# First batch with keys in one run, sums in matmuls of their own, first weights by quarters, and another order

## The chip, the cores and the metric

The kernel runs on one core of a Trainium2 chip. Its time is the device time of one execution in microseconds (us); three runs before the change gave a median of 164.9 (164.26 to 165.55).

## What is computed

```python
# q, k, v: (4, 8, 768, 64); block 32, window 16, nb = 24
k_sum = k.reshape(B, H, nb, block, D).max(axis=3)
v_sum = v.reshape(B, H, nb, block, D).mean(axis=3)
scores_l = scale * (q @ k.T)               # kept where |i - j| < window
scores_s = scale * (q @ k_sum.T) + log(block)
a = softmax(concat(masked scores_l, scores_s))
x = a @ concat(v, v_sum)                   # to (3072, 512)
out = maximum(x @ w1, x @ w2) @ w_out      # w1, w2: (512, 1024)
```

The mean times 32 equals the sum, so the factor log(32) is carried by a column of 32s beside the sums of v. The maximum is computed as relu(x(w2 - w1)) + x w1, so that out = relu(x wd) w_out + x (w1 w_out).

## The kernel before

**Tiles of work.** A batch has 768 rows, taken in three groups of 256 (`grp`), and 8 heads, taken in pairs (`hp`, 0 to 3); two pairs make a half. 64 neighbouring rows see 96 keys of their own (two windows' overhang) and the 24 key sums, so one score product has 128 rows of the array: 96 keys and 32 places for sums.

**Preparing keys** (`prep`, L594). k and q of a pair are loaded (L428), cast to `kqb` with pairs of bf16 interleaved (L593 is the helper of all copies), turned on TensorE (L624), and copied by "place k" into `kx`. There each window of 64 rows has 128 columns: 64 keys, the 32 following ("tails k"), and the 24 sums ("sums k", from the maximum of L650 in `ks`). "wrap k" copies the first 32 keys behind the last ones. One product per window (`scores`, L673, matmuls at L701) then gives both kinds of score. For some pairs of the batches 2 and 3 a DMA transpose takes the place of the turn (L628).

**Preparing values** (`load_v`, `cast_v`, `spread_v`, `sums_v`). v is loaded in 64-column pieces (L470) and cast into `vx`, which has two layouts of rows: even tiles as loaded, and odd tiles shifted by 64 rows through three copies ("odd v", parts 0 to 2). The block sums come from matmuls with `amean` (L523 for the first batch, L569 later) and are copied into rows 96 to 127 of the even layout and 32 to 63 of the odd one ("all sums"). In the first batch they go by way of two `apart` tiles: the first group of rows takes them in matmuls of their own with `apart` (L762), the other groups from `vx`.

**Weighing and values.** In the first batch the mask is laid under the scores by a matmul with `hide` ("cover", L690); later batches multiply by `mask` after the exponential (L725). The exponential is on ScalarE (L715), the products with `vx` at L757, then 1/sum (L813) and its product (L816, tile `xs`). `xs` is turned into `xt` on TensorE in the first batch (L831) and by a DMA transpose (L822) later.

**Weights and output.** w1 and w2 come in four pairs of loads of 512 KB (`load_w12`, L852). Pair n holds two of the four 128-row parts of the inner dimension, and one half of the 1024 columns. Each pair gives `wd` (the difference, L856), a bf16 cast `w1b`, its turn (L869) and `w1t`. w1o = w1 w_out is made by eight products (L897). `maxout` makes for each group four hidden products (L913), relu (L922 on ScalarE, L924 on VectorE), and for each 128 rows an output product in three parts: x with w1o (L940) and two halves of g with wo (L947); then a copy and a store. Hidden product n takes quarter (2, 0, 3, 1)[n] of the columns; n = 1 and 3 need `wd[1]` and `wd[3]`, n = 0 and 2 need `wd[0]` and `wd[2]`.

**The order.** Every operation is a numbered task, in the order in which the program creates it. Three written-out lists decide the rest: CFG["order"] is the sequence in which tasks are given out (each engine and SP's DMA queue works its own through in this sequence), CFG["engines"] has a letter per task (T TensorE, D VectorE, A ScalarE, P GpSimd, S the DMA queue of SP), and CFG["slots"] the place that each new buffer takes in its ring. The ring `land`, where loads arrive, has 13 places; a load waits in SP's queue until the last user of its place is done. On TensorE the first tasks are 14 warm-up products without use (L982). Reading the lists: a product written hidden bg.n is batch b, group g, number n; w3a and w3b are the w1 and the w2 load of weight pair 3; k12 is the keys of batch 1, pair 2.

Of the kernel before, what the change touches and what calls it, by code (L numbers as in the profile page):

```python
# [15 lines left out]
BF16 = mybir.dt.bfloat16  # L16
# [11 lines left out]
    turn="22 23 30 31 32 33", lx="SSS", cols=True, emb=1, ep=0.5, vt=0.28, s32=0.36, raw=0, qg=0, wh=1, os=6,  # L28
)
CFG["order"] = list(map(int, """  # L30
# [26 lines left out]
""".split()))  # L57
CFG["engines"] = "".join("""
PDPPPDDDPAPDPDDDDPTTTTTTTTTTTTTTSSSAAAATDDPPSSSADPATAAPPSSSPDDPTADDDSSSPDDPTADDPSSDPTASSPATDSSDATDSSPATASDSASASDDTDTAD
PPPDDTDTADPDADDTATDDPDDDPTATDDPPDDTTATDDTDTTATDDTDTTATDDTDTTATDDTDTTATDDTATTATDDTDSSSPSSSPSSSDSSSPPADAPDDDTAPDPAAPDPAT  # L60
DTDDADDDPTATDDPADDTADTDDSTADTDDSTADTDDSATPTADADADDTDTDDADAATADTDDSTADTDDSTADTDDSSSSPSSSASSSASSSPPDAPDDPPTDPPPAAAPPATDT
ADPAAAATPTADPPPDTADTDDSTADTDDSTADTDDSPSPSDDPAAASASDDPPPTADTDDSTADTDDSTADTDDSSSSPSSSPSSSASSSPPDAPDDPDTAPADPPPPPASPSDDAD
PDSDSDDPPDTADTDDSTADTDDSTADTDDSASPSADAADPSDSADAPDTADTDDSTADTDDSTADTDDSTTATTATTDTTDTDTATDTATTTDSTTTDSTATATATATTTAATTTAS
TATATDTDTTTASTTTDSTDTATDTDTTTDATTTDSTDTATATDTTTDATTTASTATDTATATTTDSTTTDSTATDTATATTTDATTTAATDTATATATTTASTTTASTATATATATT
TDSTTTAATDTDTDTDTTTDSTTTDATDTATDTDTTTDATTTASTATDTDTATTTAATTTDSTTTDSTTTAA
""".split())
CFG["slots"] = list(map(int, """
# [11 lines left out]
""".split()))  # L79
ENG = {"T": "PE", "D": "DVE", "A": "ACT", "P": "POOL", "S": "SP"}  # L80


class Ring:


    def __init__(self, slots, cap=None):
        self.slots, self.cap = slots, cap or {}
        self.owner = [None] * len(slots)
# [146 lines left out]
def kernel(  # L235
# [14 lines left out]
    nc = tc.nc  # L250
# [809 lines left out]
```

## Time and profile before

| | |
|---|---|
| median of three runs | 164.9 us |
| profiled execution | 166.2 us, span of its instructions 164.4 us |
| granted TensorE clock | 1.00 |
| TensorE matmuls busy | 153.0 us of the span, 93% |
| VectorE / ScalarE / GpSimd busy | 113.0 / 92.9 / 57.8 us |
| moved by DMA | 36.46 MB, mean 222 GB/s |

All times in the profile's rows count from the span's start. A matmul's busy time contains the latency of the pipeline, so the work of TensorE is read from the distance of starts, as the chain of waits gives it. Groups of instructions have busy time, mean time of one in ns, and the idle time ahead of them with what ended it.

### The profile page before, as it was taken

What the parts mean: (1) busy time and instruction counts of PE and PEld (TensorE: products, weight loads), DVE (VectorE), ACT (ScalarE), POOL (GpSimd) and SP (SyncE); (2) the same over time, 40 slices, a digit from 0 to 9 for tenths busy, and PEclk for the clock granted to TensorE, in tenths of its full rate; (3) what the DMA queues carried; (4) which work ended last, traced back from release to release, by engine and by line L of the source; (5) the groups of instructions that cost most, each with busy time, mean ns of one, the idle gap of its engine ahead of it and who ended that gap; (6) DMA issues with size and microseconds to landing.
All of it is one profiled execution on the core that took longest, in us unless ns stands there. A gap on an engine that the chain in (4) does not pass through costs nothing.

```text
span 164.4 us, 4431 instructions
## 1 busy us (share of the span) xinstructions
PE 153.0 (93%) x1793; PEld 100.2 (61%) x1812; DVE 113.0 (69%) x224; ACT 92.9 (57%) x134; POOL 57.8 (35%) x91
## 2 busy tenths in 40 slices
PE   5889978999999999999999999999899999999992
PEld 2346657998565644575687646678545467766651
DVE  3698898579856899994989986569746654163221
ACT  3469995794577698836996645283937312012010
POOL 6058757302242385534672546034630000000000
PEclk9999999999999999999999999999999999999999
DMA  5999999999999999999979997997999996311015
GB/s 157 289 331 303 273 386 383 383 382 371 274 190 289 271 233 219 130 232 136 201 169 229 228 209 162 121 261 150 220 245 335 319 174 167 58 64 70 0 66 189
DMA packets 67700, 36.46 MB, mean 222 GB/s; under 512 B 54624, under 2 KB 61664, under 8 KB 67680
## 3 DMA queue, kind: packets, MB, share of 16 engines
q1 hardware_dynamic: 66208, 33.76, 87.6%
q10 hardware_dynamic: 1472, 2.43, 4.4%
q8 instruction: 14, 0.23, 0.6%
q14 instruction: 6, 0.05, 0.1%
HBM read 25.17 MB, written 6.29 MB: 191 GB/s over the span
## 4 chain that ended last, share of the span: by engine, by line
PE 62%; DMA 14%; DVE 11%; issue 4%; SPq 4%; ACT 2%; POOL 1%; ACTq 0%; POOLq 0%; DVEq 0%
PE banks L913 19%; PE banks L947 17%; PE banks L940 10%; DMA land<-in_k_dram 8%; DMA out_dram<-o 6%; PE banks L897 4%; PE banks L624 3%; PE banks L757 3%; DVE vx L593 3%; PE banks L701 2%; PE banks L982 2%; DVE ks L650 2%; DVE pb L725 2%; DVE kqb L593 1%; SPq L428 1%
## 5 line engine op out<-in xcount | busy, mean ns | idle before, releaser
L913 PE MATMUL banks<-xt,wd 128*128 128x256 bf16 x384 | 45.9, 273 | 0.1
L947 PE MATMUL banks<-wo,g 128*128 128x512 bf16 (+2 forms) x194 | 43.4, 362 | 1.8 <-issue 1.6
L913 PEld LDWEIGHTS <-wd 128*128 128x128 bf16 x384 | 37.3, 98 | 7.8 <-issue 0.5
L947 PEld LDWEIGHTS <-g 128*128 128x128 bf16 x208 | 18.7, 98 | 17.3
L715 ACT ACTIVATE pb<-banks 128x1024 bf16<-128x1024 f32 x24 | 23.6, 1026 | 6.2 <-PE banks L701 3.8
L940 PE MATMUL banks<-w1o,xt 128*128 128x512 bf16 (+2 forms) x100 | 23.5, 362 | 0.2
L922 ACT ACTIVATE g<-banks 128x512 bf16<-128x512 f32 x27 | 15.2, 604 | 7.6 <-PE banks L913 7.6
L924 DVE TENSOR_SCALAR g<-banks 128x512 bf16<-128x512 f32 x21 | 14.1, 686 | 7.8 <-PE banks L913 7.6
L816 DVE TENSOR_TENSOR xs<-banks,inv 128x512 bf16<-128x512 f32 x24 | 16.0, 686 | 4.9 <-DMA xt<-xs 4.4
L593 POOL COPY vx<-sums 32x792 bf16<-32x792 bf16 x15 | 14.7, 983 | 12.5 <-ACT sums L593 7.0
L725 DVE TENSOR_TENSOR pb<-pb,mask 128x1024 bf16<-128x1024 bf16 (+1 forms) x24 | 16.4, 710 | 4.0 <-ACT pb L715 3.7
L593 ACT COPY o<-banks 128x512 f32<-128x512 f32 (+1 forms) x8 | 4.4, 546 | 25.6 <-PE banks L947 21.1
L593 POOL CAST kqb<-land 128x768 bf16<-128x768 f32 x9 | 8.9, 985 | 20.1 <-DMA land<-in_q_dram 9.8
L940 PEld LDWEIGHTS <-xt 128*128 128x128 bf16 x104 | 9.9, 98 | 9.4
L650 DVE TENSOR_REDUCE ks<-kx 128x24 bf16<-128x768 bf16 x16 | 15.0, 945 | 0.2
L593 DVE COPY o<-banks 128x512 f32<-128x512 f32 (+2 forms) x10 | 6.2, 621 | 10.2 <-PE banks L947 8.7
L593 POOL CAST vx<-land 128x768 bf16<-128x768 f32 x10 | 8.9, 889 | 10.2 <-DMA land<-in_v_dram 10.2
L593 ACT CAST kqb<-land 128x768 bf16<-128x768 f32 x11 | 10.3, 943 | 3.2 <-DMA land<-in_k_dram 2.5
L593 DVE CAST kqb<-land 128x768 bf16<-128x768 f32 x12 | 7.0, 590 | 7.1 <-DMA land<-in_k_dram 4.7
L624 PE MATMUL banks<-ident,kqb 128*128 128x128 f32 x60 | 9.7, 278 | 1.4 <-DVE kqb L593 1.1
L757 PEld LDWEIGHTS <-pb 128*64 128x64 bf16 (+1 forms) x384 | 8.0, 110 | 4.9 <-issue 2.8
L757 PE MATMUL banks<-vx,pb 128*64 128x65 bf16 (+1 forms) x384 | 9.5, 196 | 1.3 <-DVE xs L816 0.8
(87 smaller groups left out, 183.1 us busy)
## 6 DMA issues: line engine op xcount, KB each, us to landing
land<-in_k_dram SPq DMA_DIRECT2D x16, 384.0 KB, 6.0
land<-in_v_dram SPq DMA_DIRECT2D x16, 384.0 KB, 6.9
land<-in_q_dram SPq DMA_DIRECT2D x16, 384.0 KB, 5.9
land<-in_moe_w_dram SPq DMA_DIRECT2D x8, 512.0 KB, 9.6
land<-in_moe_w_out_dram SPq DMA_DIRECT2D x4, 512.0 KB, 10.0
out_dram<-o SPq DMA_DIRECT2D x7, 256.0 KB, 4.0
out_dram<-o ACTq DMA_DIRECT2D x4, 256.0 KB, 2.8
out_dram<-w1t SPq DMA_DIRECT2D x3, 256.0 KB, 3.4
```

The source lines that it names most:

```text
L593: {"D": nc.vector.tensor_copy, "A": nc.scalar.copy, "P": nc.gpsimd.tensor_copy}[e](out=o, in_=i)
L624: nc.tensor.transpose(out=bank(ps)[:, 128 * j:128 * j + 128], in_=src.ap[:].bitcast(F32)[:, 128 * j:128 * j + 128], identity=ident32[:])
L650: op("D", 0.95, lambda e: nc.vector.tensor_reduce(out=ks.ap[:, 0:nb], in_=free(kt(), 128, [256, NM], [192, 2], [32, 2], [1, 32]), axis=AX. ...
L715: op("A", {"A": 1.03}, lambda e: nc.scalar.activation(out=spread(pb.ap[:, 0, 0:1], [192, 8], [128, 2], [1, 64]) if PW > 128 else spread(pb ...
L725: nc.vector.tensor_tensor(out=o, in0=o, in1=spread(mask[:, 2 * u:2 * u + 1, 0:1], [0, n], [64, 2], [1, 64]), op=ALU.mult)
L757: nc.tensor.matmul(out=o, lhsT=p[r], rhs=vx[b].ap[r, par, hp + n, 2 * grp + u, a, 0:D + 1], start=(PW == 128 or par == 0), stop=(last and ...
L816: op("D", 0.69, lambda e: nc.vector.tensor_tensor(out=x.ap[:].rearrange("p n u a d -> p n (u a) d"), in0=spread(bank_tile[:, ps.ap, 0:1], ...
L913: nc.tensor.matmul(out=bank(ps)[:, 256 * s:256 * s + 256], lhsT=wd_tile[:, quarter, c, 128 * s:128 * s + 128], rhs=x.ap[:, c, :], start=(c ...
L922: nc.scalar.activation(out=o, in_=bank(ps), func=ACT.Relu)
L924: nc.vector.tensor_scalar_max(out=o, in0=bank(ps), scalar1=0.0)
L940: nc.tensor.matmul(out=bank(ps, c1 - c0), lhsT=x.ap[:, c, sl], rhs=w1o[c].ap[:, cols], start=(c == 0), stop=False)
L947: nc.tensor.matmul(out=bank(ps, c1 - c0), lhsT=g.ap[:, f, sl], rhs=wo[f // 2].ap[:, f % 2, cols], start=False, stop=(f == FC - 1))
```

## The change

For the first batch: keys stay in one run of 768 columns with 32 behind them ("wrap k"), without tails and without sums in `kx`; a window's product covers 96 rows, and the key sums get products of their own into rows 96 to 127, 256 columns each, per head and half of the array's rows. The sums of v stay in one `apart` tile, and all three groups take them in matmuls of their own. Odd tiles get the same row layout as even ones. The cover uses a new mask `hide0`.

Weight pairs 1 and 3 become quarters: all four inner parts of 256 columns, so that hidden product 1 needs pair 1 alone, and 3 pair 3 alone. Pairs 0 and 2 stay halves. Runs in memory are 1 KB in place of 2 KB for the quarters.

The three lists are new: which engine does a copy, the order on each engine, and the order of the loads (k and q of the first batch before its v). The number of warm-up products is the same. The diff has more settings (`f32`, `mx1`, a transpose issued by ScalarE) that are off.

```diff
-... emb=1, ..., wh=1, os=6,
+... emb=0, ..., wh=2, os=6, f32="", ft=0.7, mx1=0, ksep=1, sd=0.56,
...
+    uni = CFG["ksep"]
+    apart = tiles("apart", 1 if uni else 2, [128, H, VW], BF16) * (2 if uni else 1)
+    ksr = Ring(tiles("ks", 5 if CFG["ksep"] else 3, [128, 32], BF16))
...
-        for g in () if CFG["raw"] else (0, 2):
+        for g in () if CFG["raw"] or uni else (0, 2):
...
+            op("D", {"D": 0.17, "P": 0.3}, lambda e: on(e).tensor_copy(
+                out=hide0[:], in_=spread(hide[:, 0, 0:1], [0, 3], [1, 64])), ..., label="hide first")
+            op("D", ..., lambda e: wrap_first(e), ..., label="hide first wrap")
...
+                     runs(slice((r.start + 64) % 128, (r.start + 64) % 128 + r.stop - r.start) if uni and not late else r, 1, m0, m1),
...
-            for i, (t, r) in enumerate(zip(apart, (slice(64, 128), slice(0, 64)))):
+            for i, (t, r) in enumerate(zip(apart, (slice(96, 128),) if uni else (slice(64, 128), slice(0, 64)))):
...
+        apart_k = CFG["ksep"] and b == 0
-            pairs(128, 192, 64), order(kps, ...)
+            kt()[:, 0:S] if apart_k else pairs(128, 192, 64), order(kps, ...)
...
+        if not apart_k:
+            copy(tail_on, ..., label=f"tails k{tag}")
+            copy("D", ..., label=f"sums k{tag}")
...
-                            nc.tensor.matmul(out=bank(ps, second=a)[:, at + n0:at + n1],
-                                             lhsT=kx[b, hp + n].ap[r, 128 * t + 128:128 * t + 256],
+                            nc.tensor.matmul(out=bank(ps, second=a)[0:96 if apart_k else 128, at + n0:at + n1],
+                                             lhsT=kx[b, hp + n].ap[r, 64 * t:64 * t + 96] if apart_k else
+                                             kx[b, hp + n].ap[r, 128 * t + 128:128 * t + 256],
...
+            for n in range(2 if apart_k else 0):
+                c0 = GT * grp + 16
+                for c, at, size in ((c0, 0, min(GT, S - c0)), (0, S - c0, GT - S + c0)):
+                    for a in range(2 if size > 0 else 0):
+                        r = slice(64 * a, 64 * a + 64)
+                        nc.tensor.matmul(out=bank(ps, second=a)[96:128, GT * n + at:GT * n + at + size],
+                                         lhsT=ksum[b, hp + n].ap[r, 0:32], rhs=q_of(n, r, c, c + size), start=False,
+                                         stop=(n == 1 and at + size == GT))
...
-                        r = slice(0, 96 if par == 0 and not last else 128)
+                        r = slice(0, 96 if (par == 0 or uni) and not last else 128)
...
+    def load_w12_quarter(n, prios, prio, prio_t):
+        at_q = n // 2
+        cols, fs = slice(256 * at_q, 256 * at_q + 256), []
+            op("S", 1.47, lambda e, f=f, w=w: nc.sync.dma_start(
+                out=landed(f, KC, 256), in_=w.rearrange("(c p) n -> p c n", p=128)[:, :, cols]), ...)
+        op(CFG["wd"][n], ..., lambda e: on(e).tensor_tensor(
+            out=wd_tile[:, at_q], in0=landed(fs[1], KC, 256), in1=landed(fs[0], KC, 256), op=ALU.subtract), ...)
...
-            op("T", 0.87, lambda e, hid=hid: hid(), read=[x, wd[n % 2], wd[n % 2 + 2]], ...)
+            op("T", 0.87, lambda e, hid=hid: hid(), read=[x, wd[n]] if CFG["wh"] == 2 and n % 2 else [x, wd[n % 2], wd[n % 2 + 2]], ...)
...
-        load_w12(n, CFG["w"][2 * n:2 * n + 2], CFG["wdp"] + 10 * n, CFG["wt"])
+        (load_w12_quarter if CFG["wh"] == 2 and n % 2 else load_w12)(n, ...)
```

In the new lists the first loads are k01, k00, q01, q00, q03, k03, k02, q02, v01, v00, v03, v02, w3a, w2a, w3b, w1a, w1b, w2b, w0a, w0b, wo0, k12, wo1, k13, wo2, q11, wo3, k11 (before: k01, k00, k02, v01, v00, q01, k03, q00, q03, q02, v02, v03, w3a, w3b, w1a, w1b, k12, w2a, w0a, k10, w0b, w2b, wo1). TensorE's first products after the attention of the first batch are turn w1 1, hidden 00.3, 01.3, 00.1, 01.1, 02.1, 02.3, 02.2, 01.2, 00.2, turn k12, hidden 00.0, 01.0, w1o, hidden 02.0, w1o, turn w1 0, w1o, and then the first w1o that needs wo3 (before: turn k12, hidden 02.3, 00.3, 02.1, turn w1 2).

More of the change, by code (lines that the diff above doesn't have):

```diff
@@ L269, in tiles @@
         return [const.tile(shape, dt, name=f"{name}{i}") for i in range(n)]
-    banks = Ring(list(range(8)), {"kq": 2, "sc": -2, "av": -2, "mm": 4})
+    banks = Ring(list(range(8)), {"kq": 2, "kf": -2, "sc": -2, "av": -2, "mm": 4})
     bank_tile = psum.tile([128, 8, 512], F32, name="banks")
@@ L595, in copy, with queue @@
         op(engine, us, fn, label=label, port=port, **kw)
+    def queue(e):
+        return nc.scalar if e == "A" else nc.sync
     def on(e):
@@ L602, in prep, with turn_wide @@
         tag = f"{b}{hp}"
-        pss = []
+        pss, wide = [], [f"{n}{tag}" in CFG["f32"] for n in "kq"]
         for n, eng in enumerate((k_on,) if CFG["qg"] and b == 0 else (k_on, q_on)):
             by_dma = f"{b}{hp}" in CFG["turn"]
+            if wide[n]:
+                f, ps = kqin[b, hp, n], Buf(banks, "kf")
+                pss.append(ps)
+                def turn_wide(f=f, ps=ps):
+                    for j in range(J):
+                        nc.tensor.transpose(out=spread(bank_tile[:, ps.ap, 128 * j:128 * j + 1], [1, 128])
+                                            if j < 4 else bank(ps, second=1)[:, 128 * (j - 4):128 * (j - 3)],
+                                            in_=landed(f, 2, J * D)[:, :, D * j:D * j + D], identity=ident32[:])
+                op("T", CFG["ft"], lambda e, turn=turn_wide: turn(), read=[f], write=[ps], prio=prio, label=f"turn {'kq'[n]}{tag}")
+                continue
             f, src, ps = kqin[b, hp, n], Buf(kqb), Buf(ktr) if by_dma else Buf(banks, "kq")
@@ L751, in mm @@
                     at = 4 * a + 2 * n + u
-                    last = b > 0 or CFG["emb"] and grp > 0
+                    last = b > 0 or bool(CFG["emb"]) and grp > 0
                     for par in range(2):
@@ L878, in load_w12, with turn @@
              read=[ps], write=[w1t, w1t_part[n]], touch=weights_held, prio=prio_t, port=False, label=f"w1t {n}")
+    def load_w12_quarter(n, prios, prio, prio_t):
+        at_q = n // 2
+        cols, fs = slice(256 * at_q, 256 * at_q + 256), []
+        for w, at in zip((moe_w1, moe_w2), prios):
+            f = Buf(land)
+            fs.append(f)
+            op("S", 1.47, lambda e, f=f, w=w: nc.sync.dma_start(
+                out=landed(f, KC, 256), in_=w.rearrange("(c p) n -> p c n", p=128)[:, :, cols]),
+               write=[f], prio=at, label=f"load w{n}")
+        op(CFG["wd"][n], {"D": 1.23, "P": 2.35}, lambda e: on(e).tensor_tensor(
+            out=wd_tile[:, at_q], in0=landed(fs[1], KC, 256), in1=landed(fs[0], KC, 256), op=ALU.subtract),
+           read=fs, write=[wd[n]], prio=prio, port=True, label=f"wd {n}")
+        copy(CFG["w1b"][n], {"P": 1.05, "A": 1.05, "D": 0.69}, lambda: (w1b[n].ap[:], landed(fs[0], KC, 256)), read=fs[:1],
+             write=[w1b[n]], touch=weights_held, prio=prio, label=f"w1b {n}")
+        ps = Buf(banks, "x")
+        def turn():
+            for f in range(2):
+                for c in range(KC):
+                    nc.tensor.transpose(
+                        out=bank(ps, 1024, BF16)[:, (f * KC + c) * 128:(f * KC + c) * 128 + 128],
+                        in_=w1b[n].ap[:, c, 128 * f:128 * f + 128], identity=identity[:])
+        op("T", 0.45, lambda e: turn(), read=[w1b[n]], write=[ps], touch=weights_held, prio=prio_t, label=f"turn w1 {n}")
+        copy(CFG["w1t"][n], {"D": 0.7, "A": 1.02}, lambda: (
+            w1t.ap[:, 1024 * at_q:1024 * at_q + 1024], bank(ps, 1024, BF16)),
+             read=[ps], write=[w1t, w1t_part[n]], touch=weights_held, prio=prio_t, port=False, label=f"w1t {n}")
     def load_wo(n, prio):
@@ L915, in hid @@
                                          rhs=x.ap[:, c, :], start=(c == 0), stop=(c == KC - 1))
[L917 removed]
+            op("T", 0.87, lambda e, hid=hid: hid(), read=[x, wd[n]] if CFG["wh"] == 2 and n % 2 else [x, wd[n % 2], wd[n % 2 + 2]], write=[ps], prio=prio, label=f"hidden {b}{grp}{n}")
             def relu(e, quarter=quarter, ps=ps):
```

108 lines of the change are left out of this document (68 added, 40 removed), and 74 rows, old and new, of the table turn.

## Prediction

> **What bounds the kernel now.** I read the busy time by stretches first, then the chain of work that ended last, then the transfers into `land`. The first fence has stretches; its columns are TensorE (PE), weight loads, VectorE (DVE), ScalarE (ACT), GpSimd (POOL), granted clock, DMA share and GB/s; the third is TensorE's alone.
>
> ```profile
> 24.00:28.00 4.00, 3.09 (x93) 2.76 (x93) 3.67 (x10) 2.08 (x4) 3.66 (x2) 1.00 1.06 387
> 32.00:36.00 4.00, 4.00 (x45) 3.68 (x43) 2.92 (x3) 4.00 (x8) 0.00 (x0) 1.00 1.04 376
> 50.00:72.00 22.00, 21.27 (x285) 1.00 1.01 219
> 50.00:66.00 16.00, 15.59 (x185) 8.28 (x186) 13.76 (x25) 13.55 (x17) 8.09 (x13) 1.00 1.07 253
> ```
>
> TensorE is full from about 29 us on; before that VectorE is nearly full and the DMA runs at its rate. The chain (start, length, what) says what the start waits for, and prices each kind of matmul work:
>
> ```profile
> 10.63 0.34 PE banks L523 x6
> 12.68 0.43 PE banks L982 x2
> 17.55 10.09 DMA land<-in_k_dram
> 27.67 1.01 ACT kqb L593
> 28.72 0.55 PE banks L624 x3
> 29.27 2.62 PE banks L913 x24
> 31.89 0.45 PE banks L869 x8
> 33.66 0.33 PE banks L624 x3
> 46.59 1.73 PE banks L897 x8
> 49.19 0.83 PE banks L701 x52
> 69.62 0.89 PE banks L757 x48
> 77.16 0.86 PE banks L947 x4
> 161.19 0.29 DVE o L593
> ```
>
> The first hidden product (L913) starts at 29.27, held by the turn of keys that landed at 27.64 and were cast until 28.68. Its own `xt` was ready a little earlier. From these rows a unit of TensorE work costs: hidden 2.62/3 = 0.87, out 0.86 per four matmuls, w1o 0.87, turn of a k or q 0.33, turn of w1 0.45, cover 0.43 (two 512-column matmuls, as L982), scores 0.83/3 = 0.28, values 0.89/3 = 0.30, sums 0.34. The turn of an x and the values with the products of `apart` come from the order in time:
>
> ```profile
> 20.83 0.22 PE L757 MATMUL banks<-vx,pb 96*64 96x65 bf16 x2
> 21.38 0.78 PE L757 MATMUL banks<-vx,pb 128*64 128x65 bf16 x16
> 26.04 0.39 PE L831 MATMUL banks<-identity,xs 128*128 128x128 bf16 x4
> 26.26 0.61 PE L869 MATMUL banks<-identity,w1b 128*128 128x128 bf16 x8
> ```
>
> The turn takes 26.26 - 26.04 = 0.22. The 16 value products with their 16 `apart` products fill 20.83 to 21.38, 0.55, so `apart` adds 0.25.
>
> All TensorE work of the kernel is 48 hidden (41.8), 24 outs of three such units (61.9), 8 w1o (7.0), 20 turns of k and q (6.6), 4 of w1 (1.8), 6 of x (1.3), 6 covers (2.6), 24 scores (6.7), 24 values and two sets of `apart` (7.7), 7 sums (2.4): 139.8 us without the warm-up matmuls. It ends at 161.2. Before the first hidden product lie 9 turns, 6 covers, scores and values, the two `apart` sets, 4 sums, 2 turns of w1 and 6 of x: 13.1. So the work lags the clock by 29.3 - 13.1 = 16.2 there, and by 161.2 - 139.8 = 21.4 at the end. **The lag decides the time**: 16.2 us are lost before the hidden products, 5.2 after. The last copy and store (3.2 us) stay as they are.
>
> **When the loads land.** The next rows give issue times and time to landing.
>
> ```profile
> L470 SPq DMA_DIRECT2D land<-in_v_dram x2: 469/1792/3114, 9.7 to 10.2; - x2
> DMA to landing us min/median/max: 7.3/7.9/8.5
> L852 SPq DMA_DIRECT2D land<-in_moe_w_dram x1: 2547/2547/2547, 13.4 to 13.4; - x1
> DMA to landing us min/median/max: 7.9/7.9/7.9
> L852 SPq DMA_DIRECT2D land<-in_moe_w_dram x1: 419/419/419, 17.1 to 17.1; - x1
> DMA to landing us min/median/max: 8.2/8.2/8.2
> L852 SPq DMA_DIRECT2D land<-in_moe_w_dram x1: 431/431/431, 18.6 to 18.6; - x1
> DMA to landing us min/median/max: 11.6/11.6/11.6
> L428 SPq DMA_DIRECT2D land<-in_k_dram x2: 448/454/461, 0.7 to 1.3; - x2
> DMA to landing us min/median/max: 3.3/3.6/3.9
> ```
>
> The last v lands at 18.7, the one before at 17.0: 1.7 each. The first two k land at 4.1 and 5.1: 1.05 each. The first weight lands at 21.3, 2.6 after the last v, the fourth at 25.3: (25.3 - 21.3)/3 = 1.33 each, so the first one was 1.3 late. The next k (27.64) comes 2.3 after instead of 1.05, again 1.25 late; the two weights after it end at 30.2, 1.3 each. I keep two such delays in the new sum.
>
> **The change, part by part.** *Keys in one run.* Out go, for the first batch, 4 tails (0.25 on DVE, 0.5 on POOL) and 4 sum copies (0.28 on DVE, 0.5 elsewhere). In come products of the key sums in each of six scores: per head and half row 256 columns, four streams. Unknown cost: a 256-column matmul of L913 takes 0.109, so at most 0.44 if they go one by one, 0.22 if the two row halves overlap. Sixteen 64-column products in 0.28 are 0.017 each, less than the 0.027 that L913's rate asks, so they do overlap; I take 0.32. Six make 1.9. A gain is excluded, it is added work.
>
> *Sums of v apart.* Four more values get `apart` products, 4 x 0.25 = 1.0. Out go 8 copies into `vx` and 4 of the `apart` copies:
>
> ```profile
> L593 POOL COPY vx<-apart 32x528 bf16<-32x528 bf16 x5 | 3.7, 737 | 2.6 <-DVE apart L593 2.4
> L593 DVE COPY vx<-apart 32x528 bf16<-32x528 bf16 x3 | 1.2, 431 | 0.1
> L816 DVE TENSOR_TENSOR xs<-banks,inv 128x512 bf16<-128x512 f32 x24 | 16.0, 686 | 4.9 <-DMA xt<-xs 4.4
> L813 DVE RECIPROCAL inv<-banks 128x8 f32<-128x8 f32 x24 | 4.2, 191 | 5.5 <-PE banks L757 5.4
> L593 ACT CAST w1b<-land 128x1024 bf16<-128x1024 f32 x3 | 3.1, 1040 | 0.4 <-DMA land<-in_moe_w_dram 0.4
> L856 POOL TENSOR_TENSOR wd<-land,land 128x1024 bf16<-128x1024 f32 x2 | 4.7, 2358 | 0.3 <-DMA land<-in_k_dram 0.2
> L856 DVE TENSOR_TENSOR wd<-land,land 128x1024 bf16<-128x1024 f32 x2 | 2.5, 1226 | 2.0 <-DMA land<-in_moe_w_dram 1.9
> ```
>
> That is 3.7 us of POOL and 2.4 of DVE and ACT, all before the hidden products. Odd tiles as even move the same three copies to other rows and clear one `apart` tile less; the new mask adds a copy and two memsets. I cost these at nothing, since VectorE waits for loads in that stage once it has less to do: with the six x (6 x 0.88 = 5.3) after the last v of 18.7 plus its cast and copies (about 1.2) it is through at 25.2.
>
> *Weights by quarters.* Hidden .3 and .1 now each need one pair of loads instead of two. The four quarter loads have 1 KB runs instead of 2 KB. No row has such a run. A v load has 1536 runs of 256 B and takes 1.7, a k load 256 runs and 1.05: 0.65/1280 = 0.5 ns a run. A quarter has 256 runs more than a half, so I take 1.33 + 0.13 = 1.46. Bounds: 1.33 as the half, and 2.3 if it moved at the rate of v (1.7 x 512/384). [...] The k and half rows (384 KB in 1.05 and 512 KB in 1.33, 374 and 394 GB/s) show the rate still rising above 1.5 KB, so I go by the row.
>
> *The new order.* Loads now go k, q, then v, then the first weights as w3a, w2a, w3b, w1a, w1b, w2b, w0a, w0b, wo0, k12, wo1, k13, wo2, q11, wo3. The twelve first loads hold the same bytes and end at 18.7 again. Then: w3a 21.5 (1.3 late), w2a 22.8, w3b 24.3, w1a 25.7, w1b 27.2, w2b 29.8 (1.25 late), w0a 31.1, w0b 32.4. On SP's queue w0a and w0b wait for the slots of v03 and v02, free after their casts at about 18 and 19.3; four weights still stand before them then, so the DMA doesn't run dry. On ACT the casts of w1 stand ahead of the xt copies: w1a is cast until 26.8, then come two xt. On TensorE the turn of that w1 part stands ahead of the first hidden product, 26.8 + 0.45: it starts at **27.2**. wd 3 is ready (POOL, 24.3 + 2.36 = 26.7). wd 1 holds VectorE from 27.2 to 28.4, with a relu and an xt behind it that the fifth product wants at 27.2 + 4 x 0.87 = 30.7. Six products run to 32.4. The seventh needs w0b: 32.4 + 1.23 = 33.6. Until then TensorE has done 8 turns, 6 covers, 6 scores of 0.60, 6 values of 0.55, 4 sums, 3 turns of w1, 6 of x and 6 hidden: 2.6 + 2.6 + 3.6 + 3.3 + 1.4 + 1.4 + 1.3 + 5.2 = 21.4. **Lag 12.2.** From there six hidden products, three of w1o and two turns (8.6) lead to the first that asks for wo3, at 42.2; wo3 lands at 41.0 and is cast, at w1b's 1.04, by 42.0.
>
> The added 2.9 us lie under loads; if that cover were gone they would all be paid. After that the work left is that of before. For the later loss of 5.2 I take 4.9: between 50 and 66 VectorE was busy 13.76 of 16, between 50 and 72 TensorE idle for 0.7, and in the new list casts and output copies of that stage go to ACT. TensorE then ends at 139.8 + 2.9 + 12.2 + 4.9 = 159.8 instead of 161.2: **1.4 us less**. The profiled execution took 166.2 (span 164.4), 0.8% above the median of 164.9; the difference is put on the median: **163.5**.
>
> **The rivals.** *The start gains more.* If a quarter costs 1.33 and the second delay falls elsewhere, w0b lands 1.8 earlier, the start is at 26.8 and TensorE runs on without a wait: 26.8 + 5.2 - 21.4, lag 10.6. If the stage at 50 to 72 loses none of its 0.7 either, the end comes at 139.8 + 2.9 + 10.6 + 4.5 = 157.8, time 161.5. For it: VectorE has less work. Against: the two delays were there.
>
> *Nothing changes.* The gain of the start is lost again because loads of the next batch land as before (the DMA share is 1.01 to 1.07 in all four stretches): 164.9.
>
> *Slower.* The quarters move at the rate of v. Four times 2.3 - 1.46 is 3.4 us later for w0b and everything behind it: lag 15.6 at the seventh hidden product, end at 163.2, time 166.9. At 1.81 per quarter the gain is gone, above 2.2 it is slower by more than 1%. For it: the weights are the last thing waited for. Against: k with 1.5 KB runs shows nothing of the kind.
>
> *The clock falls.* Between the values and the turn of the first w1 part TensorE has only x turns to do. The first warm-up matmuls show a slow clock:
>
> ```profile
> 1.86 3.54 PE L982 MATMUL banks<-identity 128*128 128x512 bf16 x8 [1.86 <-DVE identity L328]
> 9.17 1.46 PE L982 MATMUL banks<-identity 128*128 128x512 bf16 x6
> ```
>
> 0.44 each against 0.24. If the clock fell so, hidden products would take twice as long for some 3.5 us: 1.7 lost, of which 1.1 lies in the wait for w0b anyway, so 164.1. [...] In the trace TensorE idled 0.9 of the 4 us from 24 to 28, and the hidden products ran at 0.87 right after.
>
> **How the numbers follow.** Forecast 0.42 (own range 162.6 to 164.4), larger gain 0.26, nothing 0.10, clock 0.05, slower 0.17. 163.5 is the likeliest. A measurement of this kernel tells about 1% from no change, so faster means under 163.25: the larger gain and 0.16 of the forecast, 0.42. Slower is 0.17, and 0.41 are within. The range 161.0 to 166.9 reaches half a microsecond below the larger gain and to the slower case.
>
> **What would show it.** The first hidden product at 27 instead of 29.3; a wait of about 1 us after six of them, ended by a DMA into `land` and wd; quarter loads 1.4 to 1.5 apart; scores of the first batch 0.6 long; TensorE nearly full from 34 to the end at 160. I am wrong if quarters land 2 us apart, if TensorE waits for x between 25 and 33, or if the later loss is far from 5 us.

## The result and the profile after

The changed kernel takes 172.1 us (median of 4 runs, 170.42 to 172.83) against 165.2 us for the kernel before, measured beside it (4 runs, 164.26 to 166.59). The ratio is 1.040, 95% interval 1.029 to 1.051: slower, and outside the range that was forecast. Some executions of a kernel take over 1.5% longer than its fastest; medians here are of all executions, ratios of those without the longer ones. The profiled execution took 172.46 us.

First the page of the changed kernel: its span, TensorE's busy tenths and the granted clock, in 40 slices of 4.27 us.

```profile
span 170.6 us, 4632 instructions
...
PE   4999976999999996699999999999999999999992
...
PEclk9999995699999999789999999999999999999998
```

There are two holes in TensorE (slices 6 and 7, slices 16 and 17), and at each the clock goes down. The same places by stretches; the columns are those of the first fence of the prediction, and the clock is the one behind POOL:

```profile
24.00:28.00 4.00, 1.42 (x62) 1.31 (x56) 1.00 (x3) 1.59 (x2) 2.87 (x3) 0.77 1.08 375
28.00:32.00 4.00, 4.00 (x65) 3.94 (x61) 2.87 (x7) 1.63 (x2) 2.36 (x1) 0.50 1.05 385
32.00:36.00 4.00, 4.00 (x44) 3.75 (x42) 1.98 (x3) 2.58 (x4) 0.99 (x1) 0.88 1.06 382
...
60.00:70.00 10.00, 7.31 (x118) 3.80 (x116) 8.67 (x12) 6.34 (x7) 7.82 (x9) 1.00 1.05 198
70.00:80.00 10.00, 10.00 (x144) 5.60 (x139) 7.35 (x19) 8.28 (x11) 2.54 (x4) 0.83 0.36 91
```

In the kernel before, TensorE was busy for 3.09 of the 4 us from 24 to 28, at a clock of 1.00. Now it is busy for 1.42, and at 28 to 32 it looks full only because the clock is 0.50 there: the eight products of a turn of w1 take 0.85 us instead of 0.45 (29.27 to 30.12, against 33.06 to 33.51). The chain that ended last (start, length, what) names what is behind each hole:

```profile
24.33 2.58 issue
...
33.67 7.86 PE banks L1002 x72
...
61.72 1.41 DVE pb L786 x2
63.12 1.56 DVE vx L609
66.10 1.01 DVE vx L609
67.15 1.36 DVE pb L786
68.54 1.05 DVE vx L609
70.08 3.05 PE banks L1036 x8
```

The first is "issue": for 2.58 us TensorE stands in the middle of the values of 020 and waits for nothing that the profile shows. The hidden products (L1002) begin at 33.5 instead of the forecast 27.2. The second is a run of VectorE's masks and copies, behind which output products (L1036) take 0.38 each instead of 0.22.

The loads are not it. The last three quarter loads of w3 and w1, by issue time and time to landing, land at 24.6, 26.6 and 27.9, where 24.3, 25.7 and 27.2 were forecast: less than a microsecond late.

```profile
L947 SPq DMA_DIRECT2D land<-in_moe_w_dram x3: 421/457/458, 18.3 to 19.3; - x3
...
DMA to landing us min/median/max: 6.4/7.8/8.6
```

The added products, in order of time in the changed kernel:

```profile
12.04 0.55 PE L752 MATMUL banks<-qx,kx 64*96 64x64 bf16 x16
12.51 0.39 PE L762 MATMUL banks<-qx,ks 64*32 64x256 bf16 x4
12.83 0.55 PE L752 MATMUL banks<-qx,kx 64*96 64x64 bf16 x16
```

The key sums take 12.51 to 12.83, the 0.32 that was forecast. The sixteen window products take 0.47 instead of 0.28, which was not: their weights have 96 columns now. The groups of weight loads up to 24 us, of the kernel before and of the changed one (busy, mean ns):

```profile
L701 PEld LDWEIGHTS <-kx 64*128 64x128 bf16 x104 | 1.8, 94 | 0.6 <-issue 0.3
```

```profile
L752 PEld LDWEIGHTS <-kx 64*96 64x96 bf16 x104 | 2.8, 121 | 1.0 <-issue 0.8
```

### The profile page after: what moved, and what is told of

The parts are those of the page before. It is cut to its first block, busy times and chain, and to the rows that moved or that the text cites. A ratio compares the mean times of both kernels' runs of the same rounds, so it can differ in the third digit from the quotient of the medians.

```text
span 170.6 us, 4632 instructions
## 1 busy us (share of the span) xinstructions
PE 159.9 (94%) x1908; PEld 106.3 (62%) x1908; DVE 104.4 (61%) x202; ACT 100.0 (59%) x137; POOL 58.5 (34%) x91
## 4 chain that ended last, share of the span: by engine, by line
PE 90%; DVE 5%; issue 2%; POOL 0%; POOLq 0%
PE banks L1002 25%; PE banks L1036 24%; PE banks L1029 11%; PE banks L818 5%; PE banks L752 5%; PE banks L1071 4%; PE banks L986 4%; PE banks L655 4%; DVE vx L609 3%; DVE pb L786 2%; PE banks L741 2%; PE banks L892 2%; PE banks L823 1%; PE banks L762 1%; PE banks L585 1%
## 5 line engine op out<-in xcount | busy, mean ns | idle before, releaser
L1036 PE MATMUL banks<-wo,g 128*128 128x512 bf16 (+2 forms) x208 | 47.5, 370 | 0.0
L1002 PE MATMUL banks<-xt,wd 128*128 128x256 bf16 x384 | 44.7, 273 | 0.0
L1002 PEld LDWEIGHTS <-wd 128*128 128x128 bf16 x384 | 37.3, 98 | 7.0
L1036 PEld LDWEIGHTS <-g 128*128 128x128 bf16 x208 | 19.1, 99 | 17.9 <-issue 1.1
L1013 DVE TENSOR_SCALAR g<-banks 128x512 bf16<-128x512 f32 x24 | 16.3, 688 | 22.0 <-PE banks L1002 22.0
L609 POOL CAST kqb<-land 128x768 bf16<-128x768 f32 x15 | 14.5, 967 | 24.0 <-PE banks L655 12.8
L609 POOL COPY vx<-sums 32x792 bf16<-32x792 bf16 x12 | 12.1, 1006 | 17.0 <-DVE sums L609 11.1
L786 DVE TENSOR_TENSOR pb<-pb,mask 128x512 bf16<-128x512 bf16 (+1 forms) x24 | 14.2, 618 | 2.2 <-ACT pb L776 2.2
L609 ACT COPY o<-banks 128x512 f32<-128x512 f32 (+1 forms) x11 | 6.1, 557 | 13.5 <-PE banks L1036 13.5
L874 DVE RECIPROCAL inv<-banks 128x8 f32<-128x8 f32 x24 | 4.7, 204 | 14.0 <-PE banks L818 7.4
L609 ACT COPY vx<-vx 32x1320 bf16<-32x1320 bf16 (+4 forms) x11 | 11.3, 1032 | 0.2
L1071 PE MATMUL banks<-identity 128*128 128x512 bf16 x28 | 8.5, 434 | 2.2 <-DVE apart L371 2.2
L609 POOL COPY vx<-vx 64x768 bf16<-64x768 bf16 (+5 forms) x8 | 6.4, 811 | 10.2 <-DVE vx L514 7.9
```

Source lines behind the costliest of these rows:

```text
L609: {"D": nc.vector.tensor_copy, "A": nc.scalar.copy, "P": nc.gpsimd.tensor_copy}[e](out=o, in_=i)
L786: nc.vector.tensor_tensor(out=o, in0=o, in1=spread(mask[:, 2 * u:2 * u + 1, 0:1], [0, n], [64, 2], [1, 64]), op=ALU.mult)
L1002: nc.tensor.matmul(out=bank(ps)[:, 256 * s:256 * s + 256], lhsT=wd_tile[:, quarter, c, 128 * s:128 * s + 128], rhs=x.ap[:, c, :], start=(c ...
L1013: nc.vector.tensor_scalar_max(out=o, in0=bank(ps), scalar1=0.0)
L1036: nc.tensor.matmul(out=bank(ps, c1 - c0), lhsT=g.ap[:, f, sl], rhs=wo[f // 2].ap[:, f % 2, cols], start=False, stop=(f == FC - 1))
L1071: nc.tensor.matmul(out=bank(ps), lhsT=identity[:], rhs=spread(identity[:, 0:1], [0, 4], [1, 128]), start=True, stop=True)
```

## The experiments

**Two theories.** Theory 1, for the first hole: TensorE has run out of fetched instructions. The new list puts 929 of TensorE's matmuls and weight loads ahead of the first hidden product instead of 727, most of them small. Rivals: a wait for data at that place, or the order of the loads. Theory 2, for the second hole: VectorE's chain between the sums of v of batch 1 and the values of 121. Rival: copies of another engine.

Theory 1 comes from a count. The kernel before has a small stall of this kind too, in the turn of an x at 27.9, which the prediction passed over; it is in its waits (line, what it waited for, us). Under it stands how many matmuls and weight loads TensorE had run by then:

```profile
PE banks L831 <- issue: 0.7, 1, 0.7
```

```profile
0.00:27.50 27.50, 22.93 (x351) 13.99 (x351) 21.45 (x62) 18.57 (x26) 17.35 (x36) 1.00 1.04 300
```

The changed kernel before and in its stall:

```profile
0.00:24.50 24.50, 22.10 (x350) 14.31 (x350) 13.82 (x36) 16.43 (x22) 11.90 (x27) 1.00 1.04 279
```

351 and 351 in the one, 350 and 350 in the other, at different work and 3 us apart. (With a few of the sequencer's own records it is number 705 in both; the expectations count so. Their 905 and 697 instructions ahead of the first hidden product were estimates; the traces have 929 and 727.)

**All runs.** Ratios are against the kernel before, measured on the same chip, with their 95% intervals.

| run | median us | ratio | first hidden product | first hole |
|---|---|---|---|---|
| changed kernel | 172.1 | 1.040 (1.029 to 1.051) | 33.5 | 2.58, issue |
| e1 sums of v back | 170.7 | 1.029 (1.022 to 1.036) | 30.8 | 1.69, GpSimd |
| e2 more instructions | 173.4 (one run) | | 34.5 | 3.16 and 1.29, issue |
| e3 loads held | 171.7 | 1.039 (1.033 to 1.044) | 33.1 | 2.14, issue |
| e4 sums on ScalarE | 168.9 | 1.019 (1.011 to 1.027) | 33.4 | 2.51, issue |
| e5 sums of v in rows | 170.9 | 1.031 (1.022 to 1.040) | 32.7 | 2.53, VectorE |
| e6 e5 and e4 | 169.2 | 1.022 (1.015 to 1.030) | 32.9 | 2.18, issue |
| e7 before, quarters alone | 165.7 | 0.999 (0.995 to 1.004) | 29.4 | 0.72, k12 |
| e8 loads held longer | 174.6 (one run) | | 34.9 | 3.77, w1 |
| e9 e4 and a pause | 171.3 | 1.035 (1.029 to 1.040) | 35.3 | 4.25, w1 |
| e10 e6 and a pause | 170.2 | 1.028 (1.021 to 1.034) | 35.1 | 5.07, w1 |
| e11 before, early products | 166.0 | 0.999 (0.994 to 1.004) | 29.2 | 1.23, issue |
| e12 e4, fewer instructions | 165.3 | 0.999 (0.994 to 1.003) | 29.5 | 0.80, w1 |

**e2: more instructions, same work.**

```diff
-            for _ in range(2):
-                nc.tensor.matmul(out=bank(ps), lhsT=identity[:], rhs=spread(identity[:, 0:1], [0, 4], [1, 128]),
+            for i in range(4):
+                nc.tensor.matmul(out=bank(ps)[:, 256 * (i % 2):256 * (i % 2) + 256], lhsT=identity[:],
+                                 rhs=spread(identity[:, 0:1], [0, 2], [1, 128]),
```

> The changed kernel, with each of the 14 warm-up tasks as four products of 256 columns instead of two of 512: the same work and time ahead of the first turn, 56 instructions more (28 products and 28 weight loads). Theory 1 (out of fetched instructions): the stall without a semaphore comes at the same count of TensorE's instructions, 705, so 56 instructions earlier in the program, late in the values of 002 (near 23.7 us) instead of late in those of 020; it is 2 to 3.5 us long. Rival (a wait for data or a buffer at that place of the program): the stall stays at the end of the values of 020, at 24.1 us. Time 171 to 174 us in both.

The counts in its first stall, and in a second one that the changed kernel does not have:

```profile
0.00:27.00 27.00, 22.16 (x350) 17.02 (x350) 14.09 (x36) 17.52 (x23) 14.62 (x29) 1.00 1.04 285
0.00:33.00 33.00, 27.07 (x478) 21.68 (x478) 17.45 (x44) 19.64 (x26) 17.26 (x31) 0.95 1.04 303
```

Again 350 and 350, so 56 instructions earlier in the program, and 256 instructions later it stalls once more, for 1.29 us. The place belongs to the count, not to the program. A wait for data is out.

**e3 and e8: no loads at the time of the fetch.** The fetches have a DMA queue of their own in the profile (q8, "instruction"): in the changed kernel 15 transfers with 0.25 MB together, 16 KB each, for 3816 matmuls and weight loads of TensorE, 254 to a transfer. What one of them brings is called a block here; its 256 instructions are read from the distance of the two stalls of e2. In e3 two landing places are exchanged, so that the first weight load waits for a cast:

```diff
-load w3a -> land 2; load w0b -> land 1
+load w3a -> land 1; load w0b -> land 2    (2 and 1 exchanged in all later loads)
```

> The changed kernel, with two landing buffers exchanged, so that the first weight load waits for the cast of v02 (about 20.8 us) instead of going out at 14.5 us: no load is under way from 20.1 us to about 22.5 us, when TensorE passes its 449th instruction (20.9 us) and the next block of 256 is due. Theory 1a (the fetch waits behind the loads that are out): the fetch starts within 1.5 us of that, at 21 to 22.4 us instead of 24.33; the stall near 24 us falls under 1 us, the clock stays at 1.00; all weights land 2.5 us later (w0b at 34.5), the first hidden product starts near 30 us instead of 33.5; time 167 to 170 us. Rival 1b (a block takes about 6 us whatever the loads do): fetch at 24.3 us, stall 2.3 to 2.8 us, clock halved, and the time 172 to 175 us.

It missed its aim, and its time of 171.7 us lies above the 167 to 170 of theory 1a: the loads were back at 21.5 us, TensorE passed its 449th instruction at 22.1 in this run, and up to 25.4 us, 3.3 behind that, there is no fetch among the packets. e8 holds them longer:

```diff
+        if tag == "000":
+            op("S", 0.2, lambda e: nc.sync.dma_start(out=late[:], in_=inv.ap[:]), read=[inv], write=[Buf(Ring([None]))])
...
+probe, on SP's queue ahead of load w3a
```

> The changed kernel, with one small transfer that waits for the first reciprocal (21.8 us, or 23 where everything begins 1.2 us later) put on SP's queue ahead of the first weight load: no load is under way from 20.1 us to at least 23 us, over the time at which TensorE passes its 449th instruction (20.9 to 22.1 us). Theory 1a (the fetch waits behind loads): it starts within 1.5 us of that instruction instead of 3.4; the stall at instruction 705 falls under 1 us. Rival 1b (a block takes some 6 us by itself): it starts 3 us or more behind, and the stall is 2 us or more. The weights come some 4 us later in both, so the time is 170 to 175 us.

The queues of the changed kernel between 20.9 us, when it has run 450 instructions, and 24.3 us, and then from 24.3 to 25.5 (packets, MB, share):

```profile
q1 hardware_dynamic: 1067, 1.14, 102.1%
```

```profile
q1 hardware_dynamic: 417, 0.42, 103.1%
q8 instruction: 1, 0.02, 5.6%
```

The fetch is not among the first 1067 packets; it starts at 24.33, 3.4 us after the count is reached. In e8, from 21.4 to 23.0 us, and the count of instructions at 21.5 and at 24.66:

```profile
DMA packets 1, 0.02 MB, mean 10 GB/s; under 512 B 0, under 2 KB 0, under 8 KB 0
...
q8 instruction: 1, 0.02, 4.9%
```

```profile
0.00:21.50 21.50, 19.27 (x224) 11.58 (x226) 11.64 (x30) 13.58 (x17) 10.14 (x25) 1.00 0.83 220
0.00:24.66 24.66, 22.43 (x350) 14.36 (x351) 13.56 (x36) 16.07 (x22) 10.60 (x26) 1.00 0.74 195
```

Here the fetch starts at 21.7, about 0.25 us after the 449th instruction, and TensorE runs through its 701st without a stop. So in e8 the block is asked for some 256 instructions before it is needed (449 and 705), and what makes it late elsewhere is the queue of loads: 3.4 us from the 449th instruction to the start of the fetch in the changed kernel, 4.1 in the kernel before (21.38 to 25.45), over 3.3 in e3, and about 0.25 without loads. Theory 1 holds, in the form 1a: the fetch waits behind the loads. The weights of e8 come late, so it waits 3.77 us for the turn of a w1 part instead.

**e1, e5: fewer instructions, by way of the old copies.** The sums of v go into the rows of `vx` again for the second and third group: 128 instructions fewer, 8 copies more.

```diff
-    ... cols=True, emb=0, ...
+    ... cols=True, emb=1, ...
...
+all sums v02.1, v02.0, v00.1, v00.0 on D behind "apart<-sums v00.0"
+all sums v06.1, v06.0, v04.1, v04.0 on D behind "x 001" (e1), behind "odd v06.2" (e5)
```

> The changed kernel, with the sums of v of the first batch written into the value rows again for the second and third group of slices (8 copies on VectorE, at a time when it is idle); the key sums stay in products of their own. Theory 1 (TensorE runs out of fetched instructions at the 705th recorded one, because 256 instructions now pass in 3.2 us while a block of them takes 6 us to come): 128 fewer instructions ahead of the first hidden product; the stall of 2.58 us near 24 us shrinks to 0 to 1.5 us, the clock stays at 1.00 there, the first hidden product starts at 27 to 29 us instead of 33.5; time 166.5 to 168.5 us (the second stall near 67 us stays). Rival (the stall is a wait for data, or the later order of the loads is at fault): the stall stays at 2 us or more near 24 us and the time stays at 171 to 173 us.

In e1 the last four copies stand ahead of the odd copies that read the same rows; so that part of the values is changed, and GpSimd's odd copies wait for the sums. The values waited 1.69 us for GpSimd at 25.0. The "issue" stall was gone, but behind a hole of that size in another place the clock was halved as well (mean clock 0.987 of 170.0 us, so 4.4 us at half), and the time stayed above the 166.5 to 168.5 us of theory 1. e5 mends the order.

> The first experiment mended: the sums of v go into the value rows again for the second and third group of slices, and the copies for the second half now stand behind the odd copies that read those rows, so that the values of 022 no longer wait through GpSimd. Theory 1: the 705th instruction of TensorE is reached after its block has come (26.4 to 27 us), the stall there is 0 to 1 us; no single idle time of TensorE between 20 and 27 us is over 1.5 us, the clock stays at 1.00 there; first hidden product at 27.5 to 29 us; time 167 to 169 us (second stall left in). Rival (data is late at that place whatever the number of instructions): an idle time of 2 us or more stays between 24 and 28 us and the time stays at 170 to 172.5 us.

The forecast of theory 1 missed: no time was won, since the wait is now VectorE's. Its four copies in e5, GpSimd at that time in e5, and the same four copies in e6, where GpSimd's difference of weights came a little later:

```profile
24.37 3.16 DVE L609 COPY vx<-apart 32x528 bf16<-32x528 bf16 x4
```

```profile
24.41 2.47 POOL L950 TENSOR_TENSOR wd<-land,land 128x1024 bf16<-128x1024 f32 x1 [0.29 <-DMA land<-in_moe_w_dram]
```

```profile
23.50 1.19 DVE L609 COPY vx<-apart 32x528 bf16<-32x528 bf16 x4
```

The four copies took 3.16 us with GpSimd's instruction of 2.47 beside them, and 1.19 in e6, where it began after their end (25.60).

**e4 and e6: the second hole.**

```diff
-all sums v121, all sums v120 on D
+all sums v121, all sums v120 on A, behind "all sums v130"
```

> The changed kernel, with two of the eight copies of the sums of v of batch 1 (those of the third pair of heads, which the values of 121 wait for) on ScalarE instead of VectorE. Theory 2 (the second stall, 66.9 to 69.6 us, is VectorE's chain of copies and masks between the sums of v and the values of 121): the stall of 2.69 us falls to 1 us or less, the clock no longer falls at 70.5 us; time 167.5 to 169.5 us, with the first stall unchanged. Rival (the values of 121 wait for copies of GpSimd or ScalarE just as long): the stall stays over 2 us and the time at 171 to 173 us.

The same two stretches as above, in e4:

```profile
60.00:70.00 10.00, 9.17 (x147) 4.93 (x150) 8.65 (x15) 9.87 (x11) 7.89 (x9) 1.00 1.01 193
70.00:80.00 10.00, 9.89 (x149) 7.25 (x144) 8.23 (x20) 9.85 (x15) 2.83 (x5) 1.00 0.80 171
```

TensorE is busy for 9.17 instead of 7.31 of the ten, the clock stays at 1.00, the wait of the values of 121 is 0.5 us, and the kernel is 3.2 us faster than the changed one. Theory 2 holds.

The sequence is long also because its instructions are. From 61.8 us to the end of the hole GpSimd works almost without a break. Between 61.4 and 69.6 us VectorE's copy of 32x264 took 0.86 us, against 0.21 in e4, and its mask at 67.15 took 1.36 us, against 0.67 for the one at 64.61. That GpSimd slows them is not shown: the mask at 64.61 took its 0.67 us beside a copy of GpSimd (64.39 to 66.90), and in e4 the 0.21 of the copy of 32x264 lay beside one too (64.31 to 67.58).

> The mended sums of v in rows, and the two copies of the sums of batch 1 on ScalarE, together. Theories 1 and 2: both stalls gone, the clock at 1.00 up to the end; the two gains add up: 163 to 165.5 us, level with or a little under the kernel before. Rival (the places are not independent, what is gained early is lost behind): 166 to 169 us.

The gains did not add up: 169.2. Without the long copies of VectorE the "issue" stall was back with 2.18 us, from 25.4 to 27.6, followed by two windows of half clock (mean clock 0.979 of 166.4 us, so 7.0 us at half). The rival's 166 to 169 us came nearest.

**e9 and e10: a pause in the loads as a cure.**

```diff
+        if tag == "022":
+            op("S", 0.2, lambda e: nc.sync.dma_start(out=late[:], in_=pb.ap[:, 0, 0:8]), read=[pb], write=[Buf(Ring([None]))])
...
+probe, on SP's queue ahead of load w3a
```

> The changed kernel with the two copies of the sums of batch 1 on ScalarE, and with one small transfer that waits for the exponentials of 022 (20.3 us, or 21.3 where TensorE runs 1.2 us later) on SP's queue ahead of the first weight load, so that no load is under way when TensorE passes its 449th instruction (20.9 or 22.1 us); the weights come some 2 us later. Theory: the fetch starts within 1.5 us of that instruction, no stall at instruction 705, the clock stays at 1.00 throughout; the weights' later landing costs less than the stall and the half clock did; 164.5 to 167.5 us, against 168.9 us with the copies on ScalarE alone. Rival (the later weights cost as much as the stall, and the idle time while they are awaited halves the clock just the same): 168 to 171 us.

> The same two edits, and the sums of v in rows for the second and third group of slices (128 instructions of TensorE fewer ahead of the first hidden product). Theory: no stall at instruction 705, at most one idle time over 1 us of TensorE between 20 and 32 us, while w3b is awaited; the clock at 1.00; 163 to 166 us, at or a little under the kernel before. Rival (idle time for the weights of over 2 us, clock halved): 167 to 170 us.

There was no "issue" stall in either, as expected; in e9 the fetch started at 22.3 us, when no load moved any data. The price was mis-sized: I had reckoned with weights 2 us late. In e9 the first weight load was issued at 22.1 and needed 4.8 us, landing at 26.9 instead of 21.5.

```profile
PE banks L933 <- ACT w1b L610: 4.3, 1, 4.3
```

TensorE waits 4.3 us for the cast of w1, and the clock falls there (mean clock 0.988 of 169.1 us, so 4.1 us at half). The rivals came nearest, and both runs were a little slower still.

**e12: fewer instructions and nothing in their place.**

```diff
-                    ... start=(PW == 128 or par == 0), stop=(last and (PW == 128 or par == 1)))
+                    ... start=(PW == 128 or par == 0), stop=True)
...
-                    for par in range(0 if last or PW > 128 else 2):
+                    for par in range(0):
```

> The changed kernel with the two copies of the sums of batch 1 on ScalarE, and without the 96 products (192 instructions) that add the sums of v in the first batch: this part of the computation is left out, nothing is put in its place, and all loads, copies and the other lists stay. Theory 1: about 713 of TensorE's instructions now stand ahead of the first hidden product instead of 905; the stall at instruction 705 falls in the turns of x or the first hidden product and is under 1.5 us, the clock stays at 1.00 throughout; first hidden product at 26.5 to 28.5 us; time 162 to 164.5 us, which is 4.5 to 7 us under the 168.9 us with the copies on ScalarE alone, for 1.6 us of TensorE's work left out. Rival (the first stall is no matter of instructions, or it costs no more than its own length): 166 to 168 us.

The granted clock in 40 slices, and the waits of TensorE:

```profile
PEclk9999999999999999999999999999999999999998
```

```profile
PE banks L1002 <- DVE wd L917: 1.2, 1, 1.2
PE banks L960 <- ACT w1b L609: 0.8, 1, 0.8
```

No "issue" stall, no half clock, 165.3 instead of e4's 168.9 us. That lies between the 162 to 164.5 us of theory 1 and the 166 to 168 of the rival. Of these 3.6 us, 1.5 are the 96 products left out (six times 0.25); the other 2.1 are put down to the first hole. The first hidden product came at 29.5, not at 26.5 to 28.5, since the turn of w1 waited for its cast, and six products later TensorE waited 1.2 us for the next difference. In this execution (166.97 us, 1.6 above the median) w1a landed at 27.9 and w0b at 34.4, 1.3 and 2.4 us later than in the changed kernel; why, no run shows. So without both holes, and with 1.5 us of work left out, the kernel is level with the one before, not ahead of it.

**e7 and e11: the kernel before with parts of the change.**

```diff
-    ... emb=0, ..., wh=2, ..., ksep=1, ...
+    ... emb=1, ..., wh=2, ..., ksep=0, ...        (lists of the kernel before)
...
+wd 1, w1b 0, turn k12, place k12, cast k10 behind hidden 00.3        (e11 alone)
```

> The kernel before, in its own order, with the quarter loads of the first weights alone: the first and third pair of loads bring 256 columns of all rows, and the hidden products of a quarter wait for their own difference alone. If quarters cost what halves cost (1.34 to 1.46 us each), 164.5 to 166 us, within 1% of before. Rival (runs of 1 KB are slow, 2.3 us each, or the quarters are what made the changed kernel slower): 167 us or more, with landings over 1.8 us apart.

> The kernel before with the quarter loads, and its lists changed at one place: the first two hidden products stand ahead of the second difference (w1) and of the turn of k12, so that they wait for the difference of w3 alone (26.4 us in the run with the quarters alone, where the first hidden product waited to 29.4 us for the second difference). Theory (the early hidden products are worth having where TensorE is not short of instructions, since the kernel before has some 697 ahead of them and not 900): first hidden product at 28 to 28.4 us, 1.0 to 1.4 us earlier; time 164 to 165.2 us, against 165.66 us with the quarters alone. Rival (the lead is given back at the next wait, for the later differences): 165.3 to 166.3 us.

The quarters alone do not change the time, as forecast. But a quarter costs more than a half. In e7 the four quarters land at 22.4, 23.9, 25.4 and 26.9, 1.5 us apart; the four halves in the kernel before land at 21.3, 22.6, 24.0 and 25.3, 1.35 apart. It does not show because the keys of k12, which the first hidden product waits for, come 1.05 us behind the last quarter, against 2.3 behind the last half.

Early products in the kernel before gain nothing either (166.0 us, where the theory had 164 to 165.2 and the rival 165.3 to 166.3): behind its 702nd matmul or weight load TensorE stood in "issue" for 1.23 us, and the first hidden product started at 29.2 as ever.

```profile
PE banks L892 <- issue: 1.2, 1, 1.2
```

So what stands behind that instruction waits in the kernel before as well (0.66 us there, 1.23 in e11). No version here beats the kernel before by more than the measurement tells.

## Why the prediction was wrong

*The loads*: right in the sum, in part by luck. w0b landed at 32.0 (32.4 forecast), but the last v came at 20.1 instead of 18.7, and the first weight only 1.35 behind it instead of 2.8. The quarters were right: 1.46 forecast, 1.50 in e7, against 1.35 for a half.

*Key sums and sums of v in products*: 0.32 and 0.25 were right, the window products were not: 0.19 more in each of six scores, 1.1 us. Their weight loads take 121 ns instead of 94; that this is the reason is likely but not shown. The prediction costed the added products and left the changed ones as they were.

*"The added 2.9 us lie under loads"*: this is the step that failed. The products were costed by their time. What was not counted is their instructions: 929 stand ahead of the first hidden product instead of 727, and they come in blocks that the same loads hold up. The first hidden product started at 33.5 instead of 27.2. Of these 6.3 us the stall is 2.58, and the half clock behind it about 2.8, an estimate from what the work between 26.9 and 33.0 us takes at full clock (0.033 per two value products, 0.22 and 0.45 per turn). The other 0.9 is covered both by the dearer scores and by w1a, which landed 0.9 later than forecast. In the terms of the lag, 33.5 less the 17.3 of work ahead of it is 16.2, against 12.2: the 6.3 less 1.1 for the scores, which is work, and less the forecast wait of 1.2 us for w0b, which fell away since the weights were there by then. So 4.0 remain.

*The clock* had a chance of 0.05 and a price under 1 us. The windows of 3.41 us at both holes of the changed kernel, and two of the kernel before:

```profile
22.76:26.16 3.40, 1.57 (x70) 1.35 (x67) 1.49 (x3) 2.59 (x4) 2.54 (x3) 1.00 1.09 372
26.17:29.58 3.41, 2.67 (x73) 2.61 (x74) 1.25 (x5) 0.07 (x1) 1.62 (x4) 0.50 1.06 386
29.59:32.99 3.40, 3.40 (x34) 3.40 (x33) 2.77 (x4) 2.05 (x3) 2.13 (x1) 0.50 1.05 383
33.00:36.41 3.41, 3.41 (x38) 3.12 (x37) 1.03 (x3) 2.08 (x4) 0.99 (x1) 1.00 1.06 382
...
67.13:70.54 3.41, 0.91 (x19) 0.63 (x20) 3.27 (x5) 0.42 (x1) 3.29 (x4) 1.00 0.80 205
70.55:73.95 3.40, 3.40 (x39) 1.50 (x37) 2.14 (x6) 2.58 (x5) 0.46 (x2) 0.50 0.18 37
```

```profile
22.31:25.71 3.40, 2.42 (x89) 2.01 (x88) 3.23 (x9) 3.08 (x4) 3.13 (x3) 1.00 1.07 400
25.72:29.12 3.40, 2.62 (x40) 2.26 (x39) 2.78 (x8) 1.07 (x3) 2.12 (x1) 1.00 1.04 380
```

The clock halved for whole windows of 3.41 us (6.83 us from 26.17, 3.41 from 70.54) after one in which TensorE was busy for 1.57 or 0.91 us, and not after 2.42 or 2.62. Closer together are one window of e6, followed by half clock, and one of e9, followed by full clock:

```profile
23.16:26.57 3.41, 1.70 (x78) 1.42 (x78) 3.27 (x10) 2.33 (x3) 1.72 (x2) 1.00 1.08 366
```

```profile
25.14:28.55 3.41, 1.77 (x92) 1.55 (x86) 2.46 (x7) 0.57 (x1) 1.03 (x1) 1.00 0.78 205
```

So in these windows the clock fell behind 1.70 us of work and less, and stayed behind 1.77 and more. To return took more: behind the window at 26.17 above, busy for 2.67 us at half clock, the clock stayed halved, and behind those at 29.59 and 70.55, busy for all of their 3.40, it was full again. The prediction asked for TensorE's idle time at this place, but took for it what the kernel before had there. That the first warm-up products took 0.44 us each is measured; that a slow clock was the reason is not shown, and the clock column of the kernel before has 1.00 from 0 to 4 us.

*The later loss*: forecast 4.9, measured 167.4 - 143.8 - 16.2 = 7.4 (end of TensorE, its work with the 1.1, lag at the first hidden product). 2.7 of it are the second hole and 1.7 its half clock (half of one window); the remaining 3.0 are less than the forecast. "In the new list casts and output copies of that stage go to ACT" was read from engine letters; VectorE's sequence between the sums and the values of 121, 8.2 us in a row, was not followed. e4 shows what the hole costs: 3.2 us.

*The sum*: 159.8 forecast for TensorE's end, and 4.0 + 2.5 + 1.1 more make 167.4, which is where it ends. That they add up proves nothing, since the later loss was taken as the rest. The other 1 us to the forecast time is that the profiled execution lay 1.3 over its median before, and 0.3 now.

*The rival "slower"* named the wrong mechanism (slow quarters), which e7 excludes.

What stays open is how much of e12's 2.1 us beyond the left-out work is stall and how much half clock, since no run has the one without the other. It is also less than the 5.4 us that stall and half clock take in the trace of the changed kernel; in e12 later loads took part of their place.

## What to carry to other kernels

Where many small products are put under a stage of loads, count their instructions as well as their time: here 6 us passed while loads ran from TensorE's 449th instruction to the first of the block that was fetched behind it (20.9 to 26.9 us), and the 256 between took 3.2, so TensorE stopped, at a place that is fixed by the count. An "issue" wait of an engine without a semaphore, at the same count in two kernels, is the sign, and it is worth looking for in the profile of before. In the trace of the changed kernel a hole took up to twice its length, since the clock was halved for the next window or two (2.58 and about 2.8 us at the first hole, 2.69 and 1.7 at the second). Taking a hole away won less, 2.1 us in e12 and 3.2 in e4; other waits, for casts and differences of late weights in e12 and for ScalarE's copies in e4, took part of its place. So follow the chain to the next wait before you price the gain.

## What the runs showed of the hardware

- The fetch of a block: its 16 KB take 1.07 us and the instructions run 2.58 us after it starts (24.33 to 26.91), in the changed kernel; 2.47 us in the kernel before (25.45 to 27.92).
- Weight loads of 64 rows and 96 columns take 121 ns (changed kernel), those of 64 rows and 128 columns 94 ns (before).
- Quarter loads with runs of 1 KB land 1.50 us apart (e7), halves with runs of 2 KB 1.35 (before), 512 KB each.
- Four copies of VectorE beside a tensor operation of GpSimd took 3.16 us (e5), and 1.19 without it (e6). In the kernel before two `xs` products beside the same operation (25.86 to 27.15, it runs from 25.49 to 27.85) took 1.29 us together; the mean of one over all 24 is 0.69.
- After a pause the first weight load took 3.8 us (e8) and 4.8 (e9) from issue to landing. In a running stream loads took longer than that (6.4 to 8.6 us for the three rows of the changed kernel above), but the landings follow each other at 1.3 to 1.5 us.
